# A planned four-layer attention kernel: a new order by the longest way to the end, and statistics and clears moved to ScalarE

## The chip, the cores and the metric

The kernel runs on one core of a Trainium2 chip, in one launch. The metric is the time of one execution in microseconds (us) of device time, the median of three runs. The engines are named as the profile names them: PE (TensorE's matmuls; PEld are its weight loads), DVE (VectorE), ACT (ScalarE), POOL (GpSimd) and SP (SyncE, which here only issues DMAs).

## What is computed

The input x has 2048 rows of 512 bf16 values. Four residual layers follow each other, A, B, A, B, with the same weights for both As and both Bs:

```python
x = x + A(layernorm(x)); x = x + B(layernorm(x))
x = x + A(layernorm(x)); x = x + B(layernorm(x))

def A(x, wqkv, wo):          # 32 heads of 16, causal window of 256
    q, k, v = heads(x @ wqkv)
    scores = einsum("bhqd,bhkd->bhqk", q, k) * 16 ** -0.5
    p = softmax(where(mask, scores, -1e9))      # mask: 0 <= i - j < 256
    return merge(einsum("bhqk,bhkd->bhqd", p, v)) @ wo

def B(x, wqkv, wo):          # linear attention, not causal
    q, k, v = heads(x @ wqkv)
    phi = lambda t: where(t > 0, t + 1, exp(t)) + 1e-6
    kv, z = sum_s phi(k) * v, sum_s phi(k)
    return merge(phi(q) @ kv / (phi(q) @ z + 1e-6)) @ wo
```

## The kernel before

The residual x stays in SBUF in f32 (`xres`, 16 tiles of 128 rows). Work goes in blocks of four tiles (512 rows, index `I` from 0 to 3). For each block of an A layer: layer norm of four tiles (`ln_tile`), transposes of the normalized tiles `xn` into `xnT` (by DMA, or on PE for the blocks that are waited for), projections of q, k and v (`prep`: `k_unit`, `q_unit`, `v_unit`), the attention, the output projection with the residual sum (`out_A`, line 518), and then at once the layer norm and the projections that layer B needs of this block (`b_proj`: phi of k, v, their product summed into `kvs` by `kv_unit`, and phi of q into `pqT`). So layer B's first half runs beside layer A's next block. What cannot is the end of layer B: only after the fourth block is `kvs` complete. Then `kv_final` makes `zb` and `wkv`, `norm_unit` divides `pqT` (on PE `zb` times `pqT`, on ACT a Ln and an Exp of minus it, lines 827 and 828, on DVE a product, line 831), and `p2_tile` makes the new x of a tile or, in the last layer, the output tile `ost`. Between the two A-B pairs, and at the end, this is a serial chain.

Inside an attention, `scores` is a phase of two or three pieces: score matmuls into PSUM (line 583), one or two exponentials on ACT (line 601, tile `pt`), and masks on the diagonal parts, on DVE (line 623) or POOL (line 628); `pv_group` multiplies `pt` with `vbd` (line 654). A block's attention has 27 or 32 such phases; both layers together have 246 exponentials, in one order. `vbd` and `kbd` hold v and k in block-diagonal form: `kbd` is made by a copy with a 0/1 factor (lines 538 and 540), and `vbd` is cleared once at the start (line 397, five buffers) and then written by DMA.

The order of everything is set by a planner in the kernel's own Python code. Each piece of work is an `Op` with a cost per engine that can do it, its dependencies, and a priority number. `Planner.run` goes forward in modelled time: it takes the operation that can start first, among those the one with the smaller priority, and issues its instructions to that engine. PSUM banks and SBUF buffers are rings (`Slot`, `Ring`, `Banks`). Where the model expects PE to be idle for more than `GAP`, it puts filling matmuls (`fill`, line 351) into a free bank. What the planner decides is fixed when the kernel is built; on the chip each engine works through its own instructions in order and waits on semaphores.

Statistics are taken on DVE (`bn_stats`, `bn_aggr`, lines 456 and 457), the inverse root on POOL (lines 460 and 461), and the normalized tile `xn` on DVE or POOL (lines 468 and 471). After everything a flag is read that would start a slow second network; it is not started here.

Of the kernel before, what the change touches and what calls it, by code (L numbers as in the profile page):

```python
# [38 lines left out]
BINS0 = ([RD, RE], [[(1, 1, 5), (4, 4, 2)], [(3, 3, 5), (4, 6, 2)]])  # L39
GROUPS = [(0, 1, 2), (3, 4, 5), (6, 7, 8), (9, 10, 11), (12, 13, 14), (15,)]  # L40


def bin_windows(bins):

    win = {u: [] for u in range(4)}
    for b, run in enumerate(bins):
        pos = 0
        for (j, w0, n) in run:
            w = w0
            if w % 2:  # L50
                assert pos == 0
                win[w // 2].append((b, -1, j))
                w += 1
            while w + 1 < w0 + n:
                win[w // 2].append((b, pos + w - w0, j))
                w += 2
            if w < w0 + n:
                assert pos + w - w0 == 7
                win[w // 2].append((b, pos + w - w0, j))
            pos += n  # L60
# [73 lines left out]
class Op:  # L134
    def __init__(self, n, cost, fn, prio, kind):
        self.n, self.cost, self.fn, self.prio, self.kind = n, cost, fn, prio, kind
        self.deps, self.slots, self.takes = set(), [], []
        self.after = 0.0
        self.end = None


class Planner:


    LAT = {"PE": .2, "ACT": .12, "DVE": .12, "POOL": .15, "SP": 1.5, "HBM": 0.0}
    WIN, FULL, GAP = 3.413, 3150, .45

    def __init__(self):
        self.ops = []

    def op(self, cost, fn, prio, reads=(), writes=(), deps=(), take=(), use=(), kind="", after=0.0):
        o = Op(len(self.ops), cost, fn, prio, kind)
# [9 lines left out]
        o.deps.discard(o)  # L162
        o.takes = list(take)
        o.slots = list(take) + list(use)
        for s in o.slots:
            s.users.append(o)
        self.ops.append(o)
        return o

    def run(self):  # L170
        free = {e: 0.0 for e in self.LAT}
# [4 lines left out]
        users = {}  # L176
        for o in self.ops:
            for d in o.deps:
                users.setdefault(d, []).append(o)
# [10 lines left out]
        while ready:  # L190
            best = None
            for o, t in ready.items():
# [5 lines left out]
                else:  # L198
                    f = True
                if f is None:  # L200
                    continue
                for e, c in o.cost.items():
                    c, bias = c if isinstance(c, tuple) else (c, 0.0)
                    start = max(t, free[e])
                    key = (round(start + bias, 2), o.prio, o.n)

                    if best is None or key < best[0]:
                        best = (key, o, e, start, c)
            assert best, "the plan has no operation that can start"
            _, o, e, start, c = best  # L210

            for p, t in ready.items():
                if p is o or e not in p.cost or (p.prio, p.n) >= (o.prio, o.n) or t > start + .02:
                    continue
                if any((s.ring.free_at(s, t) or (1e9,))[0] > start + .02 for s in p.takes):
                    continue
                c2 = p.cost[e]
                o, c = p, (c2[0] if isinstance(c2, tuple) else c2)
            del ready[o]
            fill = (0, 0)  # L220
            if e == "PE":
# [9 lines left out]
                if o.kind == "scores" and mode != "scores" or o.kind != "scores" and mode == "scores":  # L231
# [6 lines left out]
            o.end = start + c  # L238
# [9 lines left out]
            for u in users.get(o, ()):  # L248
                waits[u] -= 1
                if not waits[u]:  # L250
                    ready[u] = max([u.after, o.end + self.LAT[e]] + [d.seen for d in u.deps if d is not o])
# [889 lines left out]
```

## Time and profile before

| | |
|---|---|
| median of the runs | 514.31 us (514.26 to 515.84, 3 runs) |
| the profiled execution's own time | 515.63 us |
| its span, first to last instruction | 513.8 us |
| mean granted PE clock | 0.989 |
| busy | PE 466.8, DVE 379.8, ACT 386.2, POOL 277.9 us |
| moved by DMA | 22.79 MB |

The profile is of one execution. "Busy" is the time in which an engine had an instruction in work; idle time is put down to the engine or DMA whose semaphore came last. In a row of a group, the number after the bar is the busy time in us, then the mean of one instruction in ns, then the idle time of the engine before these instructions and who ended it. In a row of a timeline, the first number is the start, the second the length, both in us, and the square bracket holds the idle time before it and its releaser. A matmul's length includes its way through the array, so a row of n matmuls is longer than n times their distance by about one such way.

### The profile page before, as it was taken

Reading aid. Unit: us, or ns where it says so; the run is one execution under the profiler, and the core shown is the slowest. Engines: PE = TensorE matmul, PEld = TensorE weight load, DVE = VectorE, ACT = ScalarE, POOL = GpSimd, SP = SyncE. Lnnn points to the kernel's source line nnn. Section 1 sums busy time; section 2 is a strip of 40 time slices with the busy share of each in tenths; the row PEclk is TensorE's granted clock in tenths of the full one; section 3 lists DMA queues with packets and bytes.
Section 4 is the critical chain, followed back from the end, with each engine's and each line's share of the span. In section 5 each row is a group of like instructions: output and inputs, shape, how many; then the busy total and the mean of one; then the engine's idle time right before and its main releaser. Section 6 shows DMA issues by size and latency. Waiting matters only on the chain.

```text
span 513.8 us, 14702 instructions
## 1 busy us (share of the span) xinstructions
PE 466.8 (91%) x5724; PEld 239.0 (47%) x5802; DVE 379.8 (74%) x896; ACT 386.2 (75%) x415; POOL 277.9 (54%) x860
## 2 busy tenths in 40 slices
PE   1979999999899899899899998999979989999994
PEld 0325445554455454543344543555444545454441
DVE  6887777768667777688989877866756677767853
ACT  1567898899789899358458779798868989945860
POOL 8746557755844584330447876755564467533021
PEclk9989999999989999999999999999999999999998
DMA  8932222102210210000011124300230021000022
GB/s 256 279 70 51 62 50 48 22 3 47 61 24 1 54 32 4 2 0 1 0 34 33 33 67 74 54 13 2 55 64 12 3 53 33 1 3 1 1 82 88
DMA packets 56141, 22.79 MB, mean 44 GB/s; under 512 B 39680, under 2 KB 56064, under 8 KB 56064
## 3 DMA queue, kind: packets, MB, share of 16 engines
q1 hardware_dynamic: 55248, 20.99, 17.7%
q8 instruction: 47, 0.77, 0.6%
q10 hardware_dynamic: 816, 0.79, 0.6%
q14 instruction: 30, 0.25, 0.2%
HBM read 6.29 MB, written 2.10 MB: 16 GB/s over the span
## 4 chain that ended last, share of the span: by engine, by line
PE 66%; DVE 10%; DMA 8%; ACT 6%; POOL 5%; issue 4%; SPq 1%; POOLq 0%; DVEq 0%; ACTq 0%
PE psb L416 36%; PE psb L654 12%; PE psb L583 12%; DMA xnT<-xn 4%; PE psb L351 4%; ACT pt L601 2%; POOL pt L628 2%; DVE pqT L831 2%; DMA oT<-o_sb 2%; PE psb L776 1%; DVE ln_st L456 1%; ACT psb L827 1%; POOL xn L471 1%; DVE xres L518 1%; ACT psb L828 1%
## 5 line engine op out<-in xcount | busy, mean ns | idle before, releaser
L601 ACT ACTIVATE pt<-psb 128x1536 bf16<-128x1536 f32 (+2 forms) x246 | 285.6, 1220 | 31.9 <-PE psb L583 21.0
L628 POOL TENSOR_SCALAR_AFFINE_SELECT pt<-pt 128x192 bf16<-128x192 bf16 (+2 forms) x601 | 174.7, 323 | 121.0 <-ACT pt L601 115.4
L583 PE MATMUL psb<-qT,kbd 32*128 32x320 bf16 (+4 forms) x1440 | 98.4, 255 | 2.7 <-ACT pt L601 1.5
L654 PE MATMUL psb<-vbd,pt 128*128 128x34 bf16 x2880 | 92.3, 178 | 1.5 <-POOL pt L628 0.8
L654 PEld LDWEIGHTS <-pt 128*128 128x128 bf16 x2880 | 82.3, 96 | 23.4 <-issue 16.5
L623 DVE TENSOR_TENSOR pt<-pt,tri 128x64 bf16<-128x64 bf16 (+4 forms) x212 | 53.6, 277 | 29.0 <-ACT pt L601 28.1
L583 PEld LDWEIGHTS <-kbd 32*128 32x128 bf16 x1440 | 38.3, 92 | 71.3 <-issue 64.7
L416 PE MATMUL psb<-wB,xnT 128*128 128x512 bf16 x237 | 63.3, 383 | 7.5 <-DMA xnT<-xn 5.7
L416 PE MATMUL psb<-xnT,wA 128*128 128x512 bf16 x235 | 62.7, 384 | 6.0 <-DVE qT L403 2.9
L416 PEld LDWEIGHTS <-xnT 128*128 128x128 bf16 x384 | 32.4, 99 | 46.7 <-issue 10.5
L727 ACT ACTIVATE phi_e<-psb 128x512 bf16<-128x512 f32 x64 | 38.4, 605 | 18.0 <-PE psb L416 15.1
L456 DVE BATCH_NORM_STATS2 ln_st<-xres 128x6 f32<-128x512 f32 (+1 forms) x64 | 43.6, 681 | 2.8 <-DMA xres<-in_A_x_dram 2.6
L540 DVE TENSOR_TENSOR kbd<-psb,eo 128x512 bf16<-128x512 f32 x57 | 36.9, 682 | 10.1 <-PE psb L416 7.7
L460 POOL TENSOR_SCALAR ln_rs<-ln_mv 128x1 f32<-128x1 f32 x64 | 14.7, 230 | 54.4 <-DVE ln_mv L457 52.7
L351 PE MATMUL psb<-wA,identb 128*128 128x512 bf16 x158 | 42.3, 380 | 0.6 <-issue 0.2
L461 POOL TENSOR_TENSOR ln_rs<-ln_rs,mhalf 128x1 f32<-128x1 f32 x64 | 36.8, 575 | 5.3
L518 DVE TENSOR_TENSOR xres<-psb,xres 128x512 f32<-128x512 f32 x48 | 32.1, 680 | 9.1 <-PE psb L416 8.5
L416 PEld LDWEIGHTS <-wA 128*128 128x128 bf16 x256 | 21.9, 98 | 31.5 <-issue 11.9
L416 PE MATMUL psb<-wA,xnT 128*128 128x512 bf16 x121 | 34.1, 400 | 0.4
L416 PE MATMUL psb<-woA,oT 128*128 128x512 bf16 x118 | 31.0, 380 | 3.7 <-DMA oT<-o_sb 2.9
L416 PE MATMUL psb<-wkv,pqT 128*128 128x512 bf16 x125 | 29.6, 379 | 3.7 <-DVE ost L513 1.8
L416 PE MATMUL psb<-xnT,wB 128*128 128x512 bf16 x120 | 31.2, 380 | 0.4
(83 smaller groups left out, 476.5 us busy)
## 6 DMA issues: line engine op xcount, KB each, us to landing
vbd<-vst SPq DMA_DIRECT2D x128, 34.0 KB, 1.9
out_dram<-ost SPq DMA_DIRECT2D x16, 128.0 KB, 1.7
xres<-in_A_x_dram SPq DMA_DIRECT2D x14, 128.0 KB, 3.9
wB<-in_B_wqkv_dram SPq DMA_DIRECT2D x3, 512.0 KB, 5.2
wA<-in_A_wqkv_dram SPq DMA_DIRECT2D x2, 512.0 KB, 8.8
xnT<-xn SPq DMA_TRANSPOSE x44, 2.5
wA<-in_A_wqkv_dram ACTq DMA_DIRECT2D x1, 512.0 KB, 8.2
woA<-in_A_wo_dram SPq DMA_DIRECT2D x1, 512.0 KB, 8.4
```

Source lines behind the costliest of these rows:

```text
L351: nc.tensor.matmul(psb[:, k, :], lhsT=identb[:], rhs=wA[:, 0, D:2 * D], start=True, stop=True)
L416: nc.tensor.matmul(t["t"][:], lhsT=lhs(c), rhs=rhs(c), start=(c == 0), stop=(c == NCT - 1))
L456: nc.vector.bn_stats(t["st"][:], x())
L461: nc.gpsimd.tensor_tensor(t["rs"][:], t["rs"][:], mhalf[:, 0:1], op=ALU.pow)
L518: nc.vector.tensor_tensor(xres[:, i, :], ps()[:], x0(i) if first else xres[:, i, :], op=ALU.add)
L540: nc.vector.tensor_tensor(kbd[r][:, t, :, :, :].rearrange("p m k h -> p (m k) h"), ps()[:, hf * 256:(hf + 1) * 256].unsqueeze(2).to_broadc ...
L583: nc.tensor.matmul(A[:, x, at[x]:at[x] + w, :], lhsT=kbd[half(m)][32 * rg:32 * rg + 32, tt, m % 4, :, :], rhs=qT[I % 2][32 * rg:32 * rg + ...
L601: nc.scalar.activation(body[:, x:y, 0:pos[x], :], t["A"][:, x:y, 0:pos[x], :], ACT.Exp, scale=0.25)
L623: nc.vector.tensor_tensor(v, v, mt, op=ALU.mult)
L628: nc.gpsimd.affine_select(out=v, in_=v, compare_op=ALU.is_ge, fill=0.0, base=1 if kind == 0 else -2, pattern=[[0, n], [2 * sg, 64]], chann ...
L654: nc.tensor.matmul(t["O"][:, u, g, :, :], lhsT=PT[:, s0:s0 + 2, :], rhs=vbd[half(m)][:, m % 4, :, grp[g], :], start=(n == 0), stop=(n == l ...
L727: nc.scalar.activation(t["e"][:], ps()[:], ACT.Exp)
```

## The change

Five things change in the code.

- The planner orders by the longest way to the end. `ways` gives each operation the modelled length of the longest chain behind it; a table `PRIO`, by groups of operations (`"att.exp"`, `"B.k.proj"` and so on), shifts it, and a table `BIAS` shifts the choice between engines. An operation that is ready within 0.15 us and has a longer way goes first. Some costs of the model change as well.
- `vbd` is cleared by copies of a zero on ACT (line 462), in place of memsets on POOL and DVE.
- For 24 of the 64 layer norms (all 16 tiles of the third layer, and the last block before each layer B's end), the residual sum on DVE also gives the row's sum (line 638), and ACT takes the sum of squares (line 544, Square with accumulation); eight of these tiles are also normalized on ACT (lines 555 and 556).
- POOL becomes a choice for phi's middle step, for `kv_final`'s products and for the check of the sums; ACT for every `kbd` copy.
- In the last layer the output projections may use all eight PSUM banks, and norms and outputs are planned block by block.

```diff
-            pl.op({"POOL": 1.9, "DVE": (1.9, 2.0)},
-                  lambda e, k=k: (nc.vector if e == "DVE" else nc.gpsimd).memset(vbd[k][:], 0.0),
-                  1 + k, writes=[B("v", k, 0), B("v", k, 1)], after=5.0 + 2 * k)
+            pl.op({"ACT": 2.0}, lambda e, k=k: nc.scalar.copy(vbd[k][:].rearrange("p m h j e -> p (m h j e)"), zero[:].to_broadcast([P, 8 * NP * VW])),
+                  writes=[B("v", k, 0), B("v", k, 1)], after=2.5)
...
-    WIN, FULL, GAP = 3.413, 3150, .45
+    WIN, FULL, GAP = 3.413, 2750, .45
...
+    def ways(self):
+        nxt = 0.0
+        for o in reversed(self.ops):
+            lat = self.LAT[next(iter(o.cost))]
+            t = max([0.0] + [u.way + (0.0 if o.pe and u.pe else lat) for u in o.users])
+            if o.kind == "exp":
+                t = max(t, nxt)
+            o.way = min(o.cost.values()) + t
+            if o.kind == "exp":
+                nxt = o.way
...
+            o.key = (-(o.way + PRIO.get(o.group, 0.0)), o.n)
...
-                    key = (round(start + bias, 2), o.prio, o.n)
+                        bias = BIAS.get((o.group, e), 0.0) if len(o.cost) > 1 else 0.0
+                        key = (int((start + bias) * 100 + 100.5),) + o.key
...
+            for p, t in can:
+                if e in p.cost and p.key < o.key and max(t, free[e]) <= start + WAIT:
+                    o, at = p, max(t, free[e])
...
+WAIT = 0.15
+PRIO = {
+    "<lambda>": 1970, "lnA0.f_bn": 111, "lnA0.f_rs": -533, "lnA0.f_ap": -50, "lnA0.tr": 1013, "lnA0.f_trevac": -257,
...
+BIAS = {
+    ("lnA0.f_ap", "ACT"): 2.9, ("lnA0.f_ap", "DVE"): 36.2, ("lnA0.f_ap", "POOL"): 4.4, ("lnA0.f_trevac", "ACT"): 16.6,
...
+        def ln_by_act(key, i, by_pe):
...
+            nm = pl.op({"DVE": .1, "POOL": .4}, lambda e: (nc.vector if e == "DVE" else nc.gpsimd).tensor_scalar(lnm[:, c], lsum[:, c], -1.0 / D, None, op0=ALU.mult),
+                       reads=[B("x", i)])
...
+                nc.scalar.activation(t["xn"][:], xres[:, i, :], ACT.Square, bias=lsum[:, c], scale=-float(D), accum_out=lssq[:, c])
...
+                nc.gpsimd.tensor_scalar(lrs[:, c], lssq[:, c], 1.0 / D ** 3, EPS, op0=ALU.mult, op1=ALU.add)
+                nc.gpsimd.tensor_tensor(lrs[:, c], lrs[:, c], mhalf[:, 0:1], op=ALU.pow)
...
+                if e == "ACT":
+                    nc.scalar.mul(lssq[:, c], lnm[:, c], lrs[:, c])
+                    nc.scalar.activation(t["xn"][:], xres[:, i, :], ACT.Identity, bias=lssq[:, c], scale=lrs[:, c])
...
+                    if acc:
+                        nc.vector.scalar_tensor_tensor(out=xres[:, i, :], in0=ps(), scalar=1.0, in1=old, op0=ALU.mult, op1=ALU.add,
+                                                       accum_out=lsum[:, i:i + 1])
...
-            y = pl.op({"DVE": .32}, f2, EV, deps=[x], use=[es])
+            y = pl.op({"DVE": .32, "POOL": 1.95}, f2, deps=[x], use=[es])
...
-            return Slot(rings["ps"], size, {3: (0,), 2: (3,), 1: (5, 6, 7, 4, 3) if wide[0] else (5, 6, 7)}[size])
+            return Slot(rings["ps"], size, {3: (0,), 2: (3,), 1: ((5, 6, 7), (5, 6, 7, 4, 3), (0, 5, 2, 7, 1, 6, 4, 3))[int(wide[0])]}[size])
...
         for I in range(NI):
-            for j in range(2):
-                norm_unit(I, j, 2)
-        for i in range(NT):
-            p2_tile(i, 1.9, final=True)
+            norm_p2(I, "f")
```

Options for attention in two halves and for transposes in place (`HALVES`, `INPLACE`, `BINSH`) come with it and are off. The planner puts the instructions in another order on every engine; three places follow.

The first is DVE at the start, where the first four tiles are normalized. Before, up to the second normalization:

```order
L457 BN_AGGR ln_mv<-ln_st 128x2
L397 MEMSET vbd_148 128x2176
L308 TENSOR_SCALAR par_i<-pidx 128x1
L311 CAST eo<-par_i 128x1
L312 TENSOR_SCALAR eo<-eo 128x1
L468 TENSOR_SCALAR xn<-xres,ln_mv,ln_rs 128x512
L456 BN_STATS ln_st<-xres 128x6
L457 BN_AGGR ln_mv<-ln_st 128x2
L468 TENSOR_SCALAR xn<-xres,ln_mv,ln_rs 128x512
```

After, from the fourth tile's statistics on:

```order
L576 BN_STATS ln_st<-xres 128x6
L577 BN_AGGR ln_mv<-ln_st 128x2
L369 TENSOR_SCALAR par_i<-pidx 128x1
L372 CAST eo<-par_i 128x1
L373 TENSOR_SCALAR eo<-eo 128x1
L588 TENSOR_SCALAR xn<-xres,ln_mv,ln_rs 128x512 x4
L503 COPY xnT<-psb 128x4x128 x4
L576 BN_STATS ln_st<-xres 128x6
```

The memset is gone, the four statistics stand ahead of the four normalizations, and the four copies of the transposed tiles, which ACT had, follow on DVE. ACT has the five clears, `L462 COPY vbd<-zero`, right behind its table load.

The second is PE at the beginning of the first A layer's last attention, inside its score phases (`qT` and `kbd` are their operands). Before:

```order
L583 LDWEIGHTS kbd_153
L583 MATMUL psb<-qT_159,kbd_153 128x256
L583 LDWEIGHTS kbd_154
L583 MATMUL psb<-qT_159,kbd_154 128x320
L583 LDWEIGHTS kbd_155
L583 MATMUL psb<-qT_159,kbd_155 128x256
L351 LDWEIGHTS identb
L351 MATMUL psb<-wA,identb 128x512
```

After, at the same scores:

```order
L708 LDWEIGHTS kbd_155
L708 MATMUL psb<-qT_161,kbd_155 128x256
L708 LDWEIGHTS kbd_156
L708 MATMUL psb<-qT_161,kbd_156 128x320
L708 LDWEIGHTS kbd_157
L708 MATMUL psb<-qT_161,kbd_157 128x256
L481 LDWEIGHTS wB
L481 MATMUL psb<-xnT,wB 128x512
```

Where six filling matmuls began, the q projection of layer B for the block before now stands.

The third is DVE at the end, with the products of `norm_unit` (lines 831 and 983) and the output sums (lines 513 and 631). Before, to the last output:

```order
L831 TENSOR_TENSOR pqT<-pqT,psb 128x2x512
L403 CAST wkv<-psb 128x512 x2
L831 TENSOR_TENSOR pqT<-pqT,psb 128x2x512
L513 TENSOR_TENSOR ost<-psb,xres 128x512
L831 TENSOR_TENSOR pqT<-pqT,psb 128x2x512
L513 TENSOR_TENSOR ost<-psb,xres 128x512 x4
L831 TENSOR_TENSOR pqT<-pqT,psb 128x2x512 x2
L513 TENSOR_TENSOR ost<-psb,xres 128x512 x2
L831 TENSOR_TENSOR pqT<-pqT,psb 128x2x512
L513 TENSOR_TENSOR ost<-psb,xres 128x512 x4
```

After:

```order
L983 TENSOR_TENSOR pqT<-pqT,psb 128x2x512
L867 TENSOR_SCALAR phi_e<-phi_e 128x512
L870 SCALAR_TENSOR_TENSOR pqT<-psb,phi_e 128x512 x2
L983 TENSOR_TENSOR pqT<-pqT,psb 128x2x512 x2
L631 TENSOR_TENSOR ost<-psb,xres 128x512
L983 TENSOR_TENSOR pqT<-pqT,psb 128x2x512
L631 TENSOR_TENSOR ost<-psb,xres 128x512 x2
L983 TENSOR_TENSOR pqT<-pqT,psb 128x2x512 x2
L631 TENSOR_TENSOR ost<-psb,xres 128x512
L983 TENSOR_TENSOR pqT<-pqT,psb 128x2x512
```

The first products now stand ahead of the last phi of q, and an output follows at most two products; before, four outputs stood between the fifth product and the sixth.

More of the change, by code (lines that the diff above doesn't have):

```diff
@@ L680, in attention @@
             for k, (size, units) in enumerate(phs):
[L681 removed]
+                scores(I, bins, size, units, where)
                 for _, p in units:
@@ L806, in kv_final @@
+            transpose(lambda: kvn[:].rearrange("p t c -> p (t c)"), lambda: kvn[:], True,
+                      [d for jj in range(2) for d in B("kvn", jj).w], writes=[B("kvn", 0), B("kvn", 1)])
             for c in range(NCT):
```

477 lines of the change are left out of this document (292 added, 185 removed), and 13 rows, old and new, of tables (BIAS, PRIO).

## The prediction

> **What bounds the kernel now.** I read the page's head first (its busy shares), then the chain of waits, then a table of stages, then the timeline at the places that these point to.
>
> ```profile
> span 513.8 us, 14702 instructions
> ...
> PE 466.8 (91%) x5724; PEld 239.0 (47%) x5802; DVE 379.8 (74%) x896; ACT 386.2 (75%) x415; POOL 277.9 (54%) x860
> ```
>
> PE is nearly full, but some of it is not the network's work. The planner puts filling matmuls (line 351, into a free bank) wherever it expects PE to wait:
>
> ```profile
> L351 PE MATMUL psb<-wA,identb 128*128 128x512 bf16 x158 | 42.3, 380 | 0.6 <-issue 0.2
> ```
>
> The chain that ended last, by line:
>
> ```profile
> by line: PE psb L416 35.6%; PE psb L654 11.9%; PE psb L583 11.6%; DMA xnT<-xn 4.3%; PE psb L351 3.7%; issue 3.5%; ACT pt L601 2.2%; POOL pt L628 1.8%; DVE pqT L831 1.6%; DMA oT<-o_sb 1.6%; PE psb L776 1.5%; DVE ln_st L456 1.3%; ACT psb L827
> ```
>
> So 42.3 us of PE's 466.8 is filling, and with 513.8 - 466.8 = 47.0 idle PE is without useful work for 89 us. The chain passes through fillings for 3.7% (19.0 us). The stages show where (length, then busy us and instructions of PE, PEld, DVE, ACT, POOL, then the granted clock, the DMA share and GB/s):
>
> ```profile
> 0.00:21.60 21.60, 9.36 (x40) 4.23 (x41) 16.62 (x38) 7.08 (x12) 17.25 (x46) 1.00 0.88 276
> 21.60:65.00 43.40, 38.96 (x452) 18.02 (x459) 34.10 (x72) 30.57 (x33) 23.85 (x75) 0.96 0.39 75
> 65.00:115.00 50.00, 48.47 (x725) 25.99 (x727) 35.48 (x89) 45.02 (x45) 31.84 (x108) 1.00 0.15 31
> ...
> 205.00:232.00 27.00, 25.57 (x238) 13.73 (x240) 20.23 (x53) 12.67 (x18) 9.27 (x28) 1.00 0.00 1
> 232.00:257.00 25.00, 22.16 (x105) 9.65 (x107) 22.90 (x38) 17.53 (x19) 5.29 (x12) 1.00 0.00 1
> ...
> 400.00:449.00 49.00, 45.79 (x738) 25.60 (x743) 35.98 (x99) 45.85 (x47) 30.61 (x100) 1.00 0.11 24
> ```
>
> Inside an attention (65 to 115, 400 to 449) PE and ACT are both over 90% busy: the two share the bound, and a gap on PE there is a time in which ACT works off exponentials while the projections that could lie beside them have been used up. At the start PE is idle 12.2 of 21.6 us. Between the layers (205 to 257) ACT works only 30.2 of 52 us, and a serial chain is the bound.
>
> **The change, part by part.**
>
> *The start.* The clearing of vbd (line 397) leaves DVE and POOL:
>
> ```profile
> 6.01 1.87 DVE L397 MEMSET vbd<- 128x2176 bf16 x1 [0.40 <-issue]
> ...
> 9.52 0.38 DVE L468 TENSOR_SCALAR xn<-xres,ln_mv,ln_rs 128x512 bf16<-128x512 bf16 x1
> ...
> 10.58 1.91 POOL L397 MEMSET vbd<- 128x2176 bf16 x1
> ...
> 10.67 1.97 DVE L468 TENSOR_SCALAR xn<-xres,ln_mv,ln_rs 128x512 bf16<-128x512 bf16 x1
> ...
> 13.09 3.62 PE L416 MATMUL psb<-wA,xnT 128*128 128x512 bf16 x8
> ...
> 28.39 1.87 PE L416 MATMUL psb<-xnT,wA 128*128 128x512 bf16 x4 [2.86 <-DVE qT L403]
> ```
>
> The same normalization takes 0.38 us alone and 1.97 beside POOL's memset, and ends when that ends. DVE's own memset (1.87) and one such stretch (1.59) lie ahead of the first projection at 13.09; the 2.86 us at 28.39 are the same thing again, a qT copy behind stretched normalizations. All of it would be 6.3 us. The first projection cannot come 3.5 earlier, though: its weights are issued at 2.25 and land some 8.8 later, at 11.05, and four copies of xnT now stand on DVE, so I take 1.5 there (13.09 to about 11.6) and the whole 2.86: **-4.4** (bounds -6.3 and -1.5).
>
> ```profile
> 2.21 1.28 ACT L297 ACT_TABLE_LOAD   x1 [2.21 <-issue]
> ...
> 2.25 0.59 SPq L286 DMA_DIRECT2D wA<-in_A_wqkv_dram  x1
> ```
>
> ```profile
> wA<-in_A_wqkv_dram SPq DMA_DIRECT2D x2, 512.0 KB, 8.8
> ```
>
> The five clears now stand in ACT's line. Their price follows the exponentials' slope, (1459 - 1036)/512 = 0.83 ns per element (rows below), so 2176 elements take about 2.0 us and after a table load that ends at 3.5 the five end near 13.5. What waits behind them is ACT's first copy of V, which has its PSUM no earlier than that: nothing.
>
> *The order on PE.* In the built program the filling matmuls fall from 168 to 79: inside the eight attentions from 66 to 2, at the last attention's end and its output from 16 to 10, between the layers from 45 to 43, at the end from 41 to 24. One costs 0.216 us of PE's time:
>
> ```profile
> 204.62 2.40 ACT L601 ACTIVATE pt<-psb 128x1536 bf16<-128x1536 f32 x2
> 204.82 1.68 PE L351 MATMUL psb<-wA,identb 128*128 128x512 bf16 x7
> 207.38 2.37 ACT L601 ACTIVATE pt<-psb 128x1536 bf16<-128x1536 f32 x2 [0.36 <-PE psb L583]
> ...
> 495.16 2.97 PE L351 MATMUL psb<-wA,identb 128*128 128x512 bf16 x13
> ```
>
> (2.97 - 0.38)/12 = 0.216, with 0.38 the length of a single one. The rows at 204 show that a filling is not free: PE fills for 1.68 us, and ACT then waits 0.36 for the scores behind it. 89 fewer are **-19.2**, of which 13.8 inside the attentions. The bounds: all of it, or only 5.4, if what fills the gaps now (projections and kv sums that stood later) leaves gaps of the same length as idle time. I take all of it, because ACT, the other bound there, also gets less to do.
>
> *ACT.* The exponentials of a layer stay (300.2/2 = 150 us); what else stands between a layer's first and last one is counted from the two orders:
>
> ```profile
> L601 ACT ACTIVATE pt<-psb 128x1536 bf16<-128x1536 f32 x116 | 169.2, 1459 | 22.2 <-PE psb L583 16.1 <-POOL pt L628 4.0 <-POOL ln_rs L460 1.1
> L601 ACT ACTIVATE pt<-psb 128x1024 bf16<-128x1024 f32 x98 | 101.6, 1036 | 2.0 <-PE psb L583 1.9
> ...
> L727 ACT ACTIVATE phi_e<-psb 128x512 bf16<-128x512 f32 x64 | 38.4, 605 | 18.0 <-PE psb L416 15.1 <-DVE pqT L733 2.2 <-DVE pks L733 0.4
> ...
> L601 ACT ACTIVATE pt<-psb 128x896 bf16<-128x896 f32 x32 | 29.4, 918 | 7.8 <-POOL pt L628 4.0 <-PE psb L583 3.0 <-issue 0.5
> ...
> L827 ACT ACTIVATE psb<-psb,eps 128x1024 f32<-128x1024 f32 x16 | 17.4, 1090 | 6.6 <-PE psb L824 6.6
> ...
> L828 ACT ACTIVATE psb<-psb 128x1024 f32<-128x1024 f32 x16 | 16.1, 1008 | 0.5
> ...
> L403 ACT CAST vst<-psb 128x512 bf16<-128x512 f32 x15 | 8.9, 591 | 9.9 <-PE psb L416 9.3 <-ACT pt L601 0.7
> ...
> L538 ACT ACTIVATE kbd<-psb,eo 128x256 bf16<-128x256 f32 x14 | 6.6, 538 | 6.4 <-DVE kbd L540 3.9 <-PE psb L416 2.4
> ```
>
> In the first layer 24 phi, 9 copies and 4 halves of kbd (21.7 us at 0.605, 0.59 and 6.6/14 = 0.47) become 23 phi and one copy (14.5); in the second, 22.1 becomes 18.9, seven Squares among them. So ACT has 7.2 and 3.2 us less where it is a bound. Between the layers it gets about 16 us more (thirteen Squares, four normalizations and eight kbd halves), against 52 - 30.2 = 21.8 idle: hidden. A Square has no row; it is nearest to a phi (0.605) with the 0.08 that a bias operand adds (1.090 against 1.008), so 0.69 (bounds 0.605 and 1.09). If the cover between the layers were gone, the 24 would cost 16 us.
>
> *Layer norm.* For 24 of the 64 tiles the two statistics instructions (0.682 + 0.182 on DVE) go, and the residual sum carries a row sum. A tile's chain at a layer's end has a Square (0.69) in the place of the statistics (0.86), and for 8 tiles a normalization on ACT, which I put at 0.69 and a small product, together about 1.0 (bounds 0.605 and 1.2, two full ones), in the place of 0.55 on DVE; but four tiles no longer stand in one line on DVE (3 x 0.86 = 2.6). What the row sum adds to a residual sum (0.68) has no row: from 0 to 0.18, the small statistics instruction. The terms cancel within what I know of them, and I take 0 (bounds -2.6, the line on DVE alone, and +1.5, the dearest normalization and row sums). To this comes **+0.9**: between the layers PE's order now holds 16 matmuls of projections more and 12 of outputs fewer, at 0.216.
>
> ```profile
> L456 DVE BATCH_NORM_STATS2 ln_st<-xres 128x6 f32<-128x512 f32 x48 | 32.8, 682 | 0.2
> ...
> L518 DVE TENSOR_TENSOR xres<-psb,xres 128x512 f32<-128x512 f32 x48 | 32.1, 680 | 9.1 <-PE psb L416 8.5
> ...
> L457 DVE BATCH_NORM_AGGREGATE ln_mv<-ln_st 128x2 f32<-128x6 f32 x64 | 11.6, 182 | 3.4 <-POOL xn L471 0.5
> ...
> L468 DVE TENSOR_SCALAR xn<-xres,ln_mv,ln_rs 128x512 bf16<-128x512 f32 x15 | 8.1, 546 | 0.1
> ```
>
> The Trainium skill (VectorE: DVE Perf Modes, Two Vector instructions with no wait between them) counts an operation that also writes its accumulator as two instructions, a main one and a read. No row here shows one. By it the upper 0.18 would hold for four tiles at each layer's end, and the sum would be 8 x 0.18 = 1.4 us higher.
>
> *The rest.* Eight free banks for the last layer's outputs and norms that run ahead of them take PE's waits for an output buffer away:
>
> ```profile
> DVE ost L513 <- DMA out_dram<-ost: 4.7, 4, 1.9
> ...
> PE psb L416 <- DVE ost L513: 1.8, 4, 0.7
> ```
>
> **-1.8** (bounds -4.7, all that DVE waits, and 0). 49 more masks on DVE and 73 fewer on POOL, phi's middle step on POOL four times, and kvn there: neither engine is over 74% busy, nothing.
>
> *The sum.* -4.4 - 19.2 + 0.9 - 1.8 = -24.5. The profiled execution took 515.63 us (1.8 around its span), so 491.1; the runs' median, 514.31, lies 1.3 below it: **489.8 us**.
>
> **The rivals.**
>
> *The gaps come back.* The attentions keep their 13.8 us as waits of PE for ACT, POOL or a transposed tile. For it: the chain holds 4.3% of transposes for xnT. Against it: ACT's 10.4 us less. 489.8 + 13.8 = 503.6.
>
> *ACT's line is held up (slower).* A Square waits for a projection's sum, and all exponentials stand behind it in order. When ACT waits for a projection today, it waits about a microsecond:
>
> ```profile
> ACT vst L403 <- PE psb L416: 9.3, 9, 2.5
> ```
>
> 9.3/9 = 1.03 us. If each of the 24 Squares and 8 normalizations on ACT waits so, that is 33 us: 522.8. It decides from 0.82 us each (26.1 us, to 515.9); just under that, from 0.72, it ends within 0.3% of the time before, which is what a measurement of this kernel can tell from no change. Against it: the thirteen Squares between the layers stand where ACT is idle, and a sum waited for there is on the chain anyway.
>
> *The clock falls.* Where a filling goes and the work does not come, PE stands idle and its clock can drop. The stage from 21.6 to 65, with the 2.86 us wait, was granted 0.96: 0.04 x 43.4 = 1.7 us lost. The four longest fillings inside the attentions (6, 7, 7 and 9) are 1.3 to 1.9 us; if the gaps come back and these four cool at 1.7 each, 503.6 + 6.8 = 510.4. The Trainium skill (TensorE: Matmul & The Clock Gate, What's actually happening) has the clock halve after an idle window of about 3.4 us. By that rule none of the four is long enough.
>
> **How the numbers follow.** Forecast 0.75, between 480 (start -6.3, end -4.7, layer norm -2.6, together 7.4 below, and some of the attentions' idle time) and 499; gaps come back 0.11; clock 0.03; no change 0.04; ACT's line 0.07. Faster 0.75 + 0.11 + 0.03 = 0.89, same 0.04, slower 0.07. A range from 480 to 504 leaves out the two last, the clock and half of the gaps: about 0.2.
>
> **What would show it.** Line 415's matmuls near 79 and under 20 us busy; no normalization at the start over 0.6 us, and the first projection near 11.6; ACT above 90% in the attentions, with PE's idle time there no longer than now; Squares near 0.69 us with no long waits before them; the last output's matmuls end 25 us or less after the last layer's first Ln, against 29.4 now:
>
> ```profile
> 478.22 1.09 ACT L827 ACTIVATE psb<-psb,eps 128x1024 f32<-128x1024 f32 x1 [0.61 <-PE psb L824]
> ...
> 506.62 1.02 PE L416 MATMUL psb<-wkv,pqT 128*128 128x512 bf16 x4 [0.69 <-DVE ost L513]
> ```
>
> I am wrong if the attentions take as long as before while the fillings are gone, or if ACT's waits for PE grow by more than 10 us.

## The result and the profile after

The changed kernel takes 483.72 us (median of four runs, 481.56 to 485.22); the kernel before, run beside it, 514.53 (514.26 to 515.84). The ratio is 0.9393, 95% interval 0.9353 to 0.9433: 31 us faster. The profiled execution took 484.07 us with a span of 482.3, against 515.63 and 513.8. The page's head and the chain by line:

```profile
span 482.3 us, 14542 instructions
...
PE 447.1 (93%) x5647; PEld 232.2 (48%) x5713; DVE 367.5 (76%) x922; ACT 408.6 (85%) x465; POOL 269.2 (56%) x812
...
PE psb L481 40%; PE psb L787 14%; PE psb L708 14%; ACT pt L726 3%; POOL pt L759 2%; DMA wA<-in_A_wqkv_dram 2%; DMA xnT<-xn 2%; PE psb L913 1%; PE psb L500 1%; DMA oT<-o_sb 1%; DMA vbd<-vst 1%; DMA out_dram<-ost 1%; DMA xres<-in_A_x_dram 1%; PE psb L415 1%; ACT psb L979 1%
```

The fillings, in the table of groups:

```profile
L415 PE MATMUL psb<-wA,identb 128*128 128x512 bf16 x75 | 19.9, 379 | 0.1
```

So fillings fell from 42.3 to 19.9 us and PE's idle time from 47.0 to 35.2 (482.3 - 447.1). PE is without useful work for 55 us in place of 89: 34 us less, against a span shorter by 31.5, since the network's own matmuls take 2.6 us more. Where the gain lies is seen when the span is cut at the first and last exponential of each attention layer. The five stages are the start, layer 1's attention, the stretch between, layer 3's attention, and the end. The kernel before:

```profile
0.00:22.19 22.19, 9.95 (x48) 4.49 (x49) 17.17 (x39) 7.57 (x14) 17.75 (x47) 1.00 0.89 278
22.19:209.75 187.56, 176.33 (x2535) 92.84 (x2567) 136.66 (x344) 158.86 (x161) 110.33 (x358) 0.98 0.20 40
209.75:268.49 58.74, 54.40 (x320) 25.51 (x322) 50.90 (x102) 31.40 (x44) 17.81 (x47) 1.00 0.03 8
268.49:454.48 185.99, 176.12 (x2541) 92.63 (x2571) 135.45 (x337) 159.12 (x161) 119.21 (x387) 1.00 0.17 35
454.48:513.80 59.32, 50.01 (x296) 23.56 (x297) 39.57 (x77) 29.24 (x39) 12.81 (x24) 0.96 0.11 38
```

The kernel after:

```profile
0.00:26.31 26.31, 12.99 (x58) 5.97 (x60) 14.28 (x43) 16.79 (x20) 10.78 (x40) 1.00 0.90 265
26.31:200.44 174.13, 167.16 (x2459) 88.35 (x2486) 136.87 (x351) 152.66 (x149) 111.22 (x353) 0.97 0.19 38
200.44:256.45 56.01, 54.87 (x362) 26.93 (x365) 42.75 (x97) 46.62 (x86) 20.23 (x55) 1.00 0.05 11
256.45:426.28 169.83, 165.77 (x2481) 88.66 (x2507) 135.89 (x358) 156.93 (x162) 114.57 (x339) 1.00 0.18 37
426.28:482.30 56.02, 46.29 (x303) 22.30 (x304) 37.71 (x75) 35.64 (x55) 12.43 (x25) 0.96 0.12 40
```

The same two attentions for the filling matmuls alone, before and then after (PE's busy time is the figure behind the length):

```profile
22.19:209.75 187.56, 7.54 (x26) 2.45 (x31) 0.98 0.20 40
...
268.49:454.48 185.99, 9.21 (x34) 2.96 (x37) 1.00 0.17 35
```

```profile
26.31:200.44 174.13, 0.59 (x2) 0.20 (x2) 0.97 0.19 38
...
256.45:426.28 169.83, 0.00 (x0) 0.00 (x0) 1.00 0.18 37
```

| stage | before | after | difference | the prediction's terms there |
|---|---|---|---|---|
| start, to the first exponential | 22.19 | 26.31 | +4.1 | -1.5 |
| the two attentions | 373.55 | 343.96 | -29.6 | -13.8 - 2.86 = -16.7 |
| between the layers | 58.74 | 56.01 | -2.7 | +0.9 - 0.4 = +0.5 |
| end | 59.32 | 56.02 | -3.3 | -1.3 - 3.7 - 1.8 = -6.8 |
| sum | 513.80 | 482.30 | -31.5 | -24.5 |

The prediction's 19.2 us for fillings are split here by its own counts (6 fillings at the last attention's end are 1.3, 2 between the layers 0.4, 17 at the end 3.7), and its start into what lies before and behind the first exponential. The two attentions gave 29.6 us: 16.2 are busy time of fillings (16.75 to 0.59, each row's way through the array with it; at the prediction's 0.216 each, 64 fillings are 13.8), 10.1 are idle time of PE (11.23 + 9.87 to 6.97 + 4.06, length less busy), and 3.4 are work that now stands elsewhere. The idle time is seen in PE's waits in those two stages. Before (first layer 1, then layer 3):

```profile
PE psb L416 <- DMA xnT<-xn: 2.1, 2, 1.3
PE psb L416 <- DMA oT<-o_sb: 1.7, 1, 1.7
...
PE psb L416 <- DMA xnT<-xn: 3.6, 3, 1.4
PE psb L416 <- DMA oT<-o_sb: 1.3, 1, 1.3
```

After:

```profile
PE psb L481 <- DVE qT L468: 2.3, 1, 2.3
...
PE psb L481 <- DMA oT<-o_sb: 0.2, 1, 0.2
...
PE psb L481 <- DMA xnT<-xn: 0.9, 1, 0.9
...
PE psb L481 <- DMA oT<-o_sb: 0.4, 1, 0.4
```

PE waited 8.7 us for transposed tiles inside the attentions, and now waits 1.5. The 2.3 us for a qT copy are at 62.66 us and come from a transpose too: on DVE that copy stands behind a normalization that waited 2.90 us for a transpose to give its xn buffer back.

The start lost time, though its first half went as foretold. Four views of the kernel after, one after the other: PE's timeline, SP's, the chain, and ACT's:

```profile
11.43 3.57 PE L481 MATMUL psb<-wA,xnT 128*128 128x512 bf16 x8 [1.79 <-DMA wA<-in_A_wqkv_dram]
...
26.51 0.35 PE L708 MATMUL psb<-qT,kbd 32*128 32x320 bf16 x3 [3.79 <-ACT kbd L663]
```

```profile
16.89 2.66 SPq L684 DMA_DIRECT2D vbd<-vst  x4
```

```profile
18.95 5.99 DMA vbd<-vst
```

```profile
25.04 0.59 ACT L468 CAST vst<-psb 128x512 bf16<-128x512 f32 x1 [4.80 <-DMA vbd<-vst]
```

ACT's third copy of V needs the first of two vst buffers back. That buffer's DMAs stand on SP behind the loads of x and of layer B's weights, are issued at 16.9 us, and the last of them lands 6 us after its issue. ACT works in order, so a kbd copy and all exponentials wait behind the copy, and PE waits 3.79 us for that kbd.

The layer norms' new pieces, in the table of groups:

```profile
L544 ACT ACTIVATE xn<-xres,lsum 128x512 bf16<-128x512 f32 x24 | 17.2, 718 | 2.4 <-DVE xres L638 1.9 <-issue 0.2
...
L638 DVE SCALAR_TENSOR_TENSOR xres<-psb,xres 128x512 f32<-128x512 f32 x24 | 16.3, 690 | 4.6 <-PE psb L481 4.3
...
L556 ACT ACTIVATE xn<-xres,lssq,lrs 128x512 bf16<-128x512 f32 x8 | 6.5, 813 | 0.3
...
L544 ACT ACTIVATION_READ_ACCUMULATOR xn<-xres,lsum 128x1 f32 x24 | 4.6, 192 | 0.0
L555 ACT ACTIVATE lssq<-lnm,lrs 128x1 f32<-128x1 f32 x8 | 2.2, 280 | 0.0
L638 DVE DVE_READ_ACCUMULATOR xres<-psb,xres 128x1 f32 x24 | 2.0, 83 | 0.0
```

And the end, in PE's timeline and in DVE's waits:

```profile
471.63 2.75 PE L481 MATMUL psb<-wkv,pqT 128*128 128x512 bf16 x12 [0.16 <-DVE ost L631]
```

```profile
DVE ost L631 <- DMA out_dram<-ost: 5.1, 4, 2.5
```

The last output matmuls end at 474.4, but DVE still waits for output DMAs to give an output tile's buffer back.

### The profile page after: what moved, and what is told of

Its sections match the earlier page's. It is cut to its first block, busy times and chain, and to the rows that moved or that the text cites. A ratio compares the mean times of both kernels' runs of the same rounds, so it can differ in the third digit from the quotient of the medians.

```text
span 482.3 us, 14542 instructions
## 1 busy us (share of the span) xinstructions
PE 447.1 (93%) x5647; PEld 232.2 (48%) x5713; DVE 367.5 (76%) x922; ACT 408.6 (85%) x465; POOL 269.2 (56%) x812
## 4 chain that ended last, share of the span: by engine, by line
PE 72%; DMA 8%; ACT 7%; POOL 5%; DVE 4%; issue 3%; SPq 1%; ACTq 0%; DVEq 0%; POOLq 0%
PE psb L481 40%; PE psb L787 14%; PE psb L708 14%; ACT pt L726 3%; POOL pt L759 2%; DMA wA<-in_A_wqkv_dram 2%; DMA xnT<-xn 2%; PE psb L913 1%; PE psb L500 1%; DMA oT<-o_sb 1%; DMA vbd<-vst 1%; DMA out_dram<-ost 1%; DMA xres<-in_A_x_dram 1%; PE psb L415 1%; ACT psb L979 1%
## 5 line engine op out<-in xcount | busy, mean ns | idle before, releaser
L759 POOL TENSOR_SCALAR_AFFINE_SELECT pt<-pt 128x192 bf16<-128x192 bf16 (+2 forms) x528 | 155.9, 326 | 109.7 <-ACT pt L726 98.8
L787 PE MATMUL psb<-vbd,pt 128*128 128x34 bf16 x2880 | 88.8, 179 | 0.1
L787 PEld LDWEIGHTS <-pt 128*128 128x128 bf16 x2880 | 79.6, 96 | 18.4 <-issue 14.9
L754 DVE TENSOR_TENSOR pt<-pt,tri 128x128 bf16<-128x128 bf16 (+4 forms) x261 | 63.3, 280 | 13.4 <-ACT pt L726 13.0
L665 DVE TENSOR_TENSOR kbd<-psb,eo 128x512 bf16<-128x512 f32 x53 | 34.0, 685 | 7.2 <-PE psb L481 5.1
L481 PEld LDWEIGHTS <-wA 128*128 128x128 bf16 x256 | 22.6, 100 | 31.5 <-issue 11.2
L468 DVE CAST qT<-psb 128x512 bf16<-128x512 f32 x32 | 21.8, 689 | 13.0 <-PE psb L481 11.8
L576 DVE BATCH_NORM_STATS2 ln_st<-xres 128x6 f32<-128x512 f32 (+1 forms) x40 | 27.2, 680 | 3.8 <-DMA xres<-in_A_x_dram 3.8
L801 DVE RECIPROCAL rall<-psb 128x24 f32<-128x24 f32 (+1 forms) x48 | 13.8, 287 | 19.7 <-PE psb L787 19.3
L802 DVE TENSOR_TENSOR o_sb<-psb,rall 128x384 bf16<-128x384 f32 (+1 forms) x48 | 24.6, 513 | 1.7
L581 POOL TENSOR_TENSOR ln_rs<-ln_rs,mhalf 128x1 f32<-128x1 f32 x40 | 23.3, 582 | 3.3
```

The source lines that it names most:

```text
L468: (nc.scalar.copy if e == "ACT" else nc.vector.tensor_copy)(dst(), src())
L481: nc.tensor.matmul(t["t"][:], lhsT=lhs(c), rhs=rhs(c), start=(c == 0), stop=(c == NCT - 1))
L576: nc.vector.bn_stats(t["st"][:], x())
L581: nc.gpsimd.tensor_tensor(t["rs"][:], t["rs"][:], mhalf[:, 0:1], op=ALU.pow)
L665: nc.vector.tensor_tensor(kbd[r][:, t, :, :, :].rearrange("p m k h -> p (m k) h"), ps()[:, hf * 256:(hf + 1) * 256].unsqueeze(2).to_broadc ...
L754: nc.vector.tensor_tensor(v, v, mt, op=ALU.mult)
```

## The experiments

Theory W: a filling only marks a gap on PE; the new order has useful work for the gaps inside the attentions, and has the transposed tiles ready, so fillings and idle time go together. Rivals: a filling costs its 0.216 us wherever it stands (F); the fillings hold up PE's clock (C); or the work moved to other engines brings the gain, not the order (M). Where a kernel's order changed, its two tables were fitted anew by a search on the planner's model, so a few us between such kernels can also be the fit.

### Fillings left out of the kernel before and after

```diff
         def fill(k, n):
-            for _ in range(n):
+            for _ in range(0):
```

> The kernel before with its order unchanged and all 168 fillings left out (nothing of the network is left out). Theory W (a filling only marks a gap; what counts is the work that takes its place): the gap stays as idle time of PE, so at most the overshoot goes, 0.36 us behind a filling of 1.68, a fifth of 42.3 = 9 us: 505 to 515. Rival F (a filling costs its 0.216 us as the prediction's sum has it, replaced or not): 168 x 0.216 = 36 us less, 478. Rival C (the fillings hold the clock up): granted clock below 0.97 and 517 or more.

> The kernel after with its order unchanged and its 79 fillings left out. W: 64 of the 79 stand between the layers and at the end, where a serial chain is the bound: 480 to 485. F: 79 x 0.216 = 17 us less, 467. C: PE cools in the gaps of these two serial chains, projections and products there take longer: 488 or more with a granted clock below 0.96.

Before without fillings: 528.1 us (526.09 to 535.73, beside 510.07 to 519.54 for the kernel before; ratio 1.0261, interval 1.0199 to 1.0323), slower. After without fillings: 489.18 (487.88 to 491.08; ratio to the kernel before 0.9541, 0.9493 to 0.9588), slower than with them. The kernel before without fillings, its stages between the layers and at the end, and PE's longest wait in the first of them; then the end of the kernel after without fillings:

```profile
208.85:273.00 64.15, 52.05 (x287) 24.04 (x288) 51.43 (x102) 31.51 (x44) 17.48 (x45) 0.85 0.03 7
...
463.25:527.00 63.75, 44.31 (x248) 20.49 (x248) 40.18 (x77) 29.53 (x39) 12.88 (x25) 0.85 0.11 35
```

```profile
254.86 0.61 PE L416 MATMUL psb<-wkv,pqT 128*128 128x512 bf16 x2 [2.18 <-DVE pqT L831]
```

```profile
424.37:486.10 61.73, 42.40 (x270) 19.62 (x270) 37.60 (x75) 35.85 (x55) 12.42 (x25) 0.89 0.11 36
```

In the kernel before, both serial stretches lose their clock (1.00 to 0.85, 0.96 to 0.85) and grow by 5.4 and 4.4 us; layer 1's attention, which lost 7.5 us of fillings, gets only 0.9 shorter (186.65), layer 3's 4.3 longer at a clock of 0.95. F is refuted: taking a filling out without other work in its place is worth nothing, or less. W's times (505 to 515, and 480 to 485) were missed too, because a filling is more than a mark: C holds for the serial stretches of the kernel before. For the kernel after, C's time came (489) but the mean clock was 0.972, against the 0.96 that C asked for; the end alone fell to 0.89 and took 5.7 us more, while the stretch between the layers took 0.4 more (56.45).

### The longest way without the tables

```diff
-PRIO = {
...
-BIAS = {
...
+PRIO = {}
+BIAS = {}
```

> The kernel after with both tables empty: the order goes by the longest way alone and every engine choice by what starts first; the check of the sums stays on DVE. Theory O (the tables' order carries the gain): over 505 us, with fillings and waits of PE inside the attentions again (more than 20 us of the two together; 13.5 us less idle and 16 us less filling were counted there between before and after). Rival M (the work moved to other engines and the longest way carry it, the tables only trim): 484 to 492, PE's idle time and fillings inside the attentions within 5 us of the kernel after.

537.42 us (531.35 to 541.93, beside 510.07 to 519.54 for the kernel before): slower. M's time is refuted, and O's numbers came. But O's reason was only part of it. Its stages of layer 1 and the attention of layer 3, and the matmuls with layer B's weights alone in the stretch between the layers; then the same matmuls in that stretch of the kernel after:

```profile
18.51:184.46 165.95, 150.23 (x2404) 83.43 (x2425) 128.39 (x365) 152.57 (x152) 95.73 (x284) 0.98 0.24 53
184.46:255.11 70.65, 67.36 (x396) 32.19 (x401) 54.54 (x117) 45.08 (x81) 30.92 (x44) 1.00 0.02 6
255.11:438.17 183.06, 164.87 (x2450) 90.19 (x2474) 133.75 (x381) 159.73 (x165) 107.37 (x311) 0.92 0.20 35
...
184.46:255.11 70.65, 31.79 (x131) 6.19 (x64) 1.00 0.02 6
```

```profile
200.44:256.45 56.01, 10.91 (x46) 1.53 (x16) 1.00 0.05 11
```

Layer 1's attention is 8 us shorter than in the kernel after, though PE is idle 15.7 us in it, with 2.0 us of fillings; layer 3's is 13 us longer, with 18.2 us idle, 4.5 of fillings and a clock of 0.92. The longest way alone runs the exponentials ahead and leaves layer B's projections for the stretch between (131 matmuls in place of 46), where nothing covers them: 70.65 in place of 56.01 us, and the end, by the same windows, 91.33 in place of 56.02. The stretch between and the end are 50 us longer than in the kernel after, the whole span 47.2. What the tables do here is, above all, keep that work beside the exponentials.

### The order alone, and the statistics alone

```diff
-            pl.op({"ACT": 2.0}, lambda e, k=k: nc.scalar.copy(vbd[k][:].rearrange("p m h j e -> p (m h j e)"), zero[:].to_broadcast([P, 8 * NP * VW])),
+            pl.op({"POOL": 1.9, "DVE": 1.9}, lambda e, k=k: (nc.vector if e == "DVE" else nc.gpsimd).memset(vbd[k][:], 0.0),
...
-                p2_tile(4 * I + u, final=part == "f", acc=part != "f")
+                p2_tile(4 * I + u, final=part == "f", acc=False)
...
-            y = pl.op({"DVE": .32, "POOL": 1.95}, f2, deps=[x], use=[es])
+            y = pl.op({"DVE": .32}, f2, deps=[x], use=[es])
...
-                wide[0] = 2
+                wide[0] = True
```

This is the order alone, in its main lines; the same is done for `out_A`'s sums, `kv_final`, the check and kbd. The other kernel has only the two lines with `acc` set to False, the check on DVE, and tables of its own.

> Only the order of the change, none of its moved work: planner by the longest way with two tables, but vbd cleared on POOL and DVE, all statistics on DVE by bn_stats, phi's middle step, kv_final's products and the check of the sums on DVE, kbd on ACT for the first block's kind alone, five free banks at the end. The tables are fitted anew to this graph, since those of the kernel after are fitted to the moved work. Theory O (the order carries the gain inside the attentions): fillings inside the attentions nearly gone, PE idle there under 12 us in the two layers together, first to last exponential 170 to 178 us in each layer, 486 to 496 in all. Rival M (less ACT work and shorter statistics carry it): the attentions stay above 182 us each, and the time above 505.

> The kernel after with the 24 layer norms' sums back on DVE (bn_stats for all 64 tiles, no Square, no row sum), the rest of the change kept, tables fitted anew. The prediction set the layer norm's move to 0 (bounds -2.6 and +1.5). If that holds, the stretch from the last exponential of a layer to the first of the next stays within 2 us of 56.0, the end within 2 us of 56.0, and the time at 482 to 488. Rival L (the move shortens the chain at each layer's end): each of the two stretches is 2.5 us or more longer, 489 or more.

The order alone: 487.76 us beside 513.8 for the kernel before (ratio 0.9491, 0.9452 to 0.9530), 26 of the 31 us. Its two attentions and its end:

```profile
22.68:193.65 170.97, 168.64 (x2540) 90.22 (x2537) 139.18 (x348) 153.55 (x148) 119.37 (x390) 1.00 0.22 43
...
247.25:416.03 168.78, 165.19 (x2493) 87.17 (x2490) 133.60 (x330) 149.64 (x139) 120.81 (x384) 0.99 0.20 38
416.03:485.60 69.57, 58.77 (x359) 27.45 (x355) 52.04 (x103) 37.87 (x56) 11.08 (x23) 0.97 0.10 32
```

PE's idle time in the attentions is 2.3 and 3.6 us, with none of the work moved; 7.0 us of fillings are left there. O is confirmed and M refuted for them. The end is 13.6 us longer than in the kernel after, but 96 matmuls with layer B's weights stand there in place of 46 (50 x 0.216 = 10.8 us). So the 4 us between this kernel and the kernel after can come from the moved work or from the other tables; no run here separates the two.

The statistics on DVE: 485.63 us (483.78 to 489.07; ratio 0.9468, 0.9419 to 0.9517). The interval overlaps that of the kernel after, so no effect of the 24 layer norms is shown. The stretch between the layers:

```profile
195.04:251.28 56.24, 51.93 (x311) 24.05 (x309) 47.49 (x95) 32.87 (x48) 19.27 (x48) 1.00 0.03 8
```

It is as long as with ACT's sums (56.01), though not with the same work: it holds 58 matmuls with layer B's weights, there 46. The end was longer (62.91), but 80 matmuls with layer B's weights stand there in place of 46 (34 x 0.216 = 7.3 us), so it cannot be compared either. Rival L is thus neither shown nor ruled out.

### The start's stall

```diff
-    for i in range(8, NT):
+    for i in range(8, 12):
         nc.sync.dma_start(x0(i), x_dram[i])
-    nc.sync.dma_start(wB[:, :, D:2 * D], wcols(B_wqkv, 1))
...
+    def load_rest():
+        for i in range(12, NT):
+            nc.sync.dma_start(x0(i), x_dram[i])
+        nc.sync.dma_start(wB[:, :, D:2 * D], wcols(B_wqkv, 1))
...
+                if m0 == 6 and key[1] == 0:
+                    load_rest()
```

> The kernel after, order on all compute engines unchanged; on SP the loads of the last four x tiles and of layer B's weights (2 MB) go behind the first block's fourth vbd DMA, where they stood ahead of the first. In the kernel after the first exponential starts at 26.31 us because ACT's third copy of V waits 4.8 us for the first vbd DMA, which SP issues at 16.9, behind those loads, and which lands 6 us after its issue. Theory S (the start's stall is this queue): the first exponential starts near 21.5 us, the wait is under 1 us, and 4 to 5 us go: 479 to 480. Rival H (hidden or given back): the loads then meet the transposes and vbd DMAs of the second block, PE or ACT waits there instead, and the time stays within 1.5 us of the kernel after, 482 to 485.

481.19 us (479.97 to 484.05; ratio 0.9370, 0.9334 to 0.9406): the interval overlaps that of the kernel after, and the median lies between S's times and H's. In the profiled execution the first exponential came at 21.60, as S says, and layer 1's last one at 200.18 against 200.44: given back, as H says. That execution took 484.05 us, 2.9 above the median, so the others may have given back less. Layer 1's attention, and PE's longest wait in it:

```profile
21.60:200.18 178.58, 166.71 (x2460) 88.39 (x2486) 136.82 (x352) 152.97 (x148) 111.41 (x353) 0.97 0.25 53
```

```profile
PE psb L485 <- DVE vst L472: 5.2, 1, 5.2
```

The same ring of vst buffers stops a later block's copy of V, now behind the moved loads. So both the ring and the loads were taken away, and the ring of output tiles at the end with them:

```diff
-        vst = [fp.tile([P, 2, NP, VW], BF, name=f"vst{k}") for k in range(2)]
+        vst = [fp.tile([P, 2, NP, VW], BF, name=f"vst{k}") for k in range(4)]
...
+            nc.gpsimd.dma_start(x0(i), x_dram[i])
+        nc.gpsimd.dma_start(wB[:, :, D:2 * D], wcols(B_wqkv, 1))
...
+                if key == ("A", 0, 1) and u == 3:
+                    load_rest()
...
-                    t["o"] = work.tile([P, D], BF, name="ost", tag=f"xn{ost.k}", bufs=1)
+                    t["o"] = kbd[i // 4][:, i % 4, :, :, :].rearrange("p m k h -> p (m k h)")
```

> The kernel after with its order on PE, ACT and DVE unchanged and two repairs. Start: the last four x tiles and layer B's weights are loaded by POOL's DMA queue after the eighth tile's statistics, in place of SP's queue ahead of the first vbd DMA, and vst has four buffers for two, so that no copy of V waits for a vbd DMA. End: the output tiles lie in kbd, which is free by then, in place of a ring of four, so that no sum waits for an output DMA (DVE 5.1, POOL 5.7, PE 0.8 us of such waits in the kernel after). Theory S (these waits are on the path): first exponential near 21.5 us and layer 1's last one near 196, 4 us ahead of the kernel after; the end 3 us shorter, near 53; 476 to 478. Rival H (given back): the last exponential of layer 1 comes at 199 or later, as in the run with late loads (200.2), and only the end's 3 us stay, 480 to 481. Rival P (issuing eight DMAs holds POOL up, and the masks behind it): ACT's waits for POOL in layer 1 grow by over 3 us, 483 or more.

488.98 us (485.6 to 492.05; ratio 0.9514, 0.9471 to 0.9557): slower than the kernel after. P's time came by a mechanism that no theory had; ACT's waits for POOL in layer 1 stayed at 8.5 us. PE's longest wait, and SP's timeline:

```profile
PE psb L485 <- DMA vbd<-vst: 10.8, 1, 10.8
```

```profile
21.62 22.42 SPq L691 DMA_DIRECT2D vbd<-vst  x12
```

Twelve small vbd DMAs took 22.4 us while 2 MB of weights, issued by POOL at 19 to 22 us, landed. Layer B needs these weights near 89 us. The next kernel differs from this one only in when they are issued:

```diff
+                if key == ("A", 0, 2) and u == 3:
+                    load_b()
```

> The kernel with both repairs and the order of the kernel after, but layer B's weights (2 MB, first needed near 89 us) are issued by POOL only after the twelfth tile's statistics, near 45 us, in place of 19 to 22 us. In the run with both repairs PE waited 10.8 us for a vbd DMA at 35 us: 12 vbd DMAs on SP took 22.4 us while those weights landed (12.7 to 15.7 us each). Theory B (the weights' transfers hold up the small vbd DMAs): the 12 take 6 to 9 us, the wait of 10.8 goes, layer 1's last exponential comes at 196 to 197 in place of 206.7, and the time is 477 to 479. Rival V (the vbd DMAs are slow by themselves at that place): a wait of 5 us or more stays at 30 to 46 us, 484 or more. Rival H (the start is given back once more, elsewhere in the first layer): last exponential at 199 or later, 480 to 483.

477.01 us (475.68 to 478.24; ratio 0.9281, 0.9245 to 0.9318): 12 us less than the kernel with the early issue, and faster than the kernel after and the kernel before. SP's timeline, then layer 1's attention and the end:

```profile
21.56 9.33 SPq L695 DMA_DIRECT2D vbd<-vst  x12
```

```profile
22.32:195.77 173.45, 165.00 (x2460) 87.72 (x2486) 137.29 (x352) 152.72 (x148) 114.28 (x357) 0.99 0.25 51
...
420.66:474.40 53.74, 46.08 (x303) 22.36 (x304) 37.71 (x75) 35.64 (x56) 12.42 (x25) 0.96 0.12 41
```

B is confirmed: the twelve DMAs take 9.3 us, the wait of 10.8 is gone, and layer 1's last exponential comes 4.7 us ahead of the kernel after. The start's stall was thus on the path, and the end's ring of output tiles cost 2.3 us (56.02 to 53.74).

### Both repairs known to the planner

The repairs enter the planner (four vst buffers, no output ring, the loads' times), costs follow the trace (Square 0.92, residual sum with row sum 0.69, normalization on ACT 1.05), and the tables are fitted to it. The second kernel moves layer B's weights as above.

> Both repairs of the other kernel, now known to the planner (four vst buffers, no ring for the outputs, the loads' real times), some of its costs set to what the trace of the kernel after shows (Square with its accumulation 0.92, the row-sum addition 0.69, a normalization on ACT 1.05, an output DMA's issue 0.6, a DMA's way 1.9 us), and the tables fitted to that. If the planner's remaining errors at the start and the end (which it does not know in the kernel after) are what separates plan and chip, this is at or under the kernel with the two repairs alone, 473 to 478. If the fit of the tables matters more than these costs, it is slower than that one, 479 to 485.

> The same move of layer B's weights in the kernel with both repairs and new tables, order otherwise as there. There PE waited 4.3 us at 32.4 for a transposed tile while those weights landed. Theory B: that wait falls under 1 us and 3 to 4 us go, 474 to 475. Rival H: the gain is given back inside the first layer, where ACT and PE are both full: within 1.5 us of 478.

477.98 us (475.7 to 479.84; ratio 0.9291, 0.9256 to 0.9327) with the weights at 18 to 21 us, in the range expected and as fast as the best one above. That one has the old tables and costs, so this does not show that the planner's costs were what was missing. With the weights at 39 to 42 us it is 481.42 (ratio 0.9377, 0.9338 to 0.9416), slower: neither theory. The chain of that kernel:

```profile
41.05 10.68 DMA xnT<-xn
```

A tile's transpose, issued while the weights land, takes 10.7 us, and PE waits 5.5 us for it. So the moved loads met another small transfer. Its first exponential also came 1.5 us later (24.41 against 22.90) with an order that is the same up to there. PE waited 1.7 us for the first weights in that execution and 0.5 in the other; only one execution of each was profiled, and why stays open.

## Why the prediction was right, and where its steps failed

The forecast was 489.8 (480 to 504); 483.72 is inside, 6 us below. The mechanism it named, order on PE, is what the runs show: the order alone brings 26 of the 31 us. But it is the order with its tables; the longest way by itself was slower than the kernel before. The sizes of four steps were off, and partly cancelled, which is luck: against the terms the attentions gave 12.9 us more and the stretch between the layers 3.2 more, the start 5.6 less and the end 3.5 less.

*The order on PE.* -13.8 inside the attentions fits the fillings that went, but PE's idle time gave 10.1 us more, and the sum had no term for it. The prediction read a gap there as time in which ACT works off exponentials, and took the chain's 4.3% of transposes as evidence for its rival that gaps come back. The waits before say otherwise: 1.5 us for ACT's `pt`, 8.7 for transposed tiles. An earlier order removes these as well: 1.5 us are left, or 3.8 with the qT copy behind a transpose. That the price of 0.216 per filling came out is right only because work took the place; left empty, the fillings' gaps gained 0.9 us in one attention and lost 4.3 in the other.

*The start.* First projection: 11.43, foretold near 11.6. The 2.86 us behind a stretched normalization went. The step that failed is the sentence on the clears, "What waits behind them is ACT's first copy of V ... nothing". The clears do end at 13.1 and the first copy is on time. It is the third copy that waits, for a vbd DMA behind SP's loads: SP's queue was not followed. So -1.5 to the first exponential became +4.1, and the run with both repairs and the weights later gets back 4.7 us by layer 1's end. Even in the runs with that stall repaired the first exponential comes at 21.60 to 22.32, against 22.19 before: the earlier projection does not reach it. ACT has ten halves of kbd and three copies of V ahead of it there, four and two before; without the tables, with four and one, it comes at 18.51. That points to the order on ACT, which no run tests alone.

*Between the layers.* +0.9 - 0.4 foretold, -2.7 measured: PE's idle time there fell from 4.3 to 1.1, which no term held.

*The end.* -6.8 foretold, -3.3 measured. Fillings gave 5.8 us in that stage, but 2.1 us of work came in, and -1.8 for eight banks missed: the ring of four output tiles kept DVE waiting 5.1 us (4.7 before). The matmuls did end 24.8 us after the last layer's first Ln (449.54 to 474.38), under the 25 foretold and 4.6 less than before, but the outputs behind them took 7.9 us in place of 6.2.

*ACT and layer norm.* 0 foretold, and no effect shown with the statistics back on DVE. Single prices: a Square is 0.718 and a read of its accumulator 0.192, so 0.91 for 0.69; a normalization 0.813 + 0.280 = 1.09 for 1.0; the row sum 0.083, inside 0 to 0.18. The Trainium skill's rule (VectorE: DVE Perf Modes, Two Vector instructions with no wait between them) that an accumulator output makes two instructions agrees with that row on DVE; ACT's rows show the same. All 24 Squares waited 2.4 us together and the eight normalizations 0.3; the rival that had each wait over 0.8 us is refuted. ACT's work in the two attentions fell by 6.2 and 2.2 us, foretold 7.2 and 3.2.

*ACT above 90% in the attentions* held in layer 3 (156.9 of 169.8) and not in layer 1 (152.7 of 174.1, 88%), where the start's stall lies.

*The clock.* It did not fall in the kernel after (0.985 against 0.989). The rival looked for it inside the attentions. Without fillings it falls, but mainly in the serial stretches. In the kernel after the 24 fillings at the end earn their place (5.7 us); the 43 between the layers made 0.4 us there.

## What to carry to other kernels

Idle time that an engine fills with dummy work is a marker, and sometimes holds the clock up: taking the dummy work out is worth nothing, or costs time, and bringing real work there is worth both the filling and the waits around it. An order that runs the bounding engine ahead is not yet good; count what it leaves uncovered for the serial stretch behind. When a step moves onto an in-order engine, follow the DMA queue that gives its buffers back, and load nothing large while small transfers are waited for.

## What the runs showed of the hardware

- The granted clock fell to 0.85 over a stretch in which PE's longest wait was 2.18 us. The Trainium skill (TensorE: Matmul & The Clock Gate, What's actually happening) ties the lower clock to an idle window of about 3.4 us; here shorter gaps, 12.1 us of the stretch's 64.15 together, were enough; with the fillings the same stretch was granted 1.00.
- Loads of 512 KB issued on POOL's queue held up 34 KB DMAs of SP's queue: twelve of them took 22.4 us beside these loads and 9.3 without. The Trainium skill (DMA: Bandwidth & Descriptors, Issuing engines are not separate DMA queues) says that queues share the same DMA engines; the two runs agree, and give the price, 12 us of kernel time.
